# A first tile of 90 rows, earlier constants, small products between the first pairs, and routing in groups of 10, 4 and 2 tiles

## The chip, the core and the metric

The kernel runs on one NeuronCore of a Trainium2 chip: TensorE (PE in the profile, its weight loads PEld), VectorE (DVE), ScalarE (ACT), GpSimd (POOL) and SyncE (SP, which here only issues DMAs). The metric is device time in microseconds of one execution; lower is better.

## The reference

Talking-heads attention over 4 batches, 12 heads, 448 positions and 64 dimensions per head: scores are mixed between heads (`w_pre`) before the softmax, and probabilities are mixed again (`w_post`) behind it. Its output, 1,792 tokens of 768, goes to a layer of 8 experts, each token to the one with the highest cosine similarity to the experts' vectors:

```python
scores = scale * np.matmul(q, k.transpose(0, 1, 3, 2))
scores = np.einsum('bhij,hg->bgij', scores, w_pre)
scores = scores - np.max(scores, axis=-1, keepdims=True)
attn = np.exp(scores)
attn = attn / (np.sum(attn, axis=-1, keepdims=True) + 1e-09)
attn = np.einsum('bhij,hg->bgij', attn, w_post)
x = matmul(attn, v)                        # 1792 tokens of 768
logits = xn @ en.T / tau                   # xn, en: rows divided by their norms
idx = argmax(logits); gate = softmax(logits)[idx]
out[idx == e] = gate * (np.maximum(x @ w1[e], 0) @ w2[e])
```

## The kernel before, in words

**Tiles and steps.** The 448 query rows of a batch are cut into tiles of 120, 120, 120 and 90 (lines 25 and 26), 16 tiles in all. For each tile and each of 6 pairs of heads, `emit_qk` multiplies q by k (line 249); ACT or DVE moves the result from PSUM to `s` (lines 256, 258) and `place` sends it by two DMAs (line 263) to a group buffer `g`, in which 10 partitions take rows of the tile for each head, so that heads lie along the partitions. There are three such buffers (line 142); `free` says from which step a tile may be placed. Then the tile is worked off in steps of 20 rows, 10 at the end of a 90-row tile: 6, 6, 6 and 5 steps, 92 over all tiles. A step is: `emit_pre` (line 283, the mix by `w_pre`), `emit_max` (line 291, DVE), `emit_exp` (line 300, ACT), `emit_r` (lines 308 to 311, the last of them the factor `wr` on POOL), `emit_post` (lines 326 and 331, the mix by `w_post`, which also transposes), and its eviction to `a` on DVE (line 339). Pre, max and exp run two steps ahead (`LEAD`).

**The order of the work** is written out by hand: every engine and every DMA queue takes its instructions in the order in which the loop of line 784 emits them, and waits come from semaphores. In the loop the head products of later tiles are put in as `due` (line 208) says: one pair a step, three in two steps near the end, all of them by step `OPEN` = 79. Behind a tile's last step, its values products (`emit_av`, line 352), the evictions to `xT` and `xs` on ACT (lines 364, 382), the logits (line 370, lines 402 to 407 on DVE), the sum of squares (line 394) and the store to `x_tok` (line 389, SP) follow in the next tile's steps (the lists `acts`, `dves`, `pes`, `avs`, `bg`).

**Ahead of the loop** (lines 746 to 777) q, k and small constants are asked for, eight small products of ones keep PE occupied, ten pairs of head products (`N0`) are made, eight more small products follow, then pre, max and exp of steps 0 and 1. The chain that divides the experts' vectors by their norms (`embed`) runs in steps 0 to 11, three pieces a step.

**Routing.** At step 79 `open_right` frees the memory of q, k and s, opens that of the weights and asks for four weight tiles. From there `early` and `gate_value` run in the loop, two and three pieces a step: the one-hot of 12 tiles (`NE`), its prefix sums on POOL, ranks, index products, and a gather of expert 0's first 128 rows. From step 80, one half of a weight tile is split per step into a high part (line 567, ACT) and a remainder (line 568, DVE). Behind the loop come the last tile's values and logits, routing of three tiles (12 to 14) and then of the last one, while expert 0's first pass (`ffn_tok`, lines 616 to 640) fills PE in portions (`SA`). The gate values of the last four tiles are worked out inside that pass (lines 934 to 941), stored to `g_tok` from ACT's queue (line 467) and gathered; then expert 0's second pass (`st_b`) and experts 1 to 7 follow.

## Time and profile before

| | |
|---|---|
| Time before | 746.73 us, median of 3 runs (736.13 to 749.99) |
| Profiled execution | 745.5 us, span 743.6 us |
| PE busy | 693.0 us (93% of the span) |
| DVE, ACT, POOL busy | 464.0, 392.1, 118.0 us |
| PE in tenths, 40 slices of 18.6 us | 6699999999999999998988969999999999999984 |
| PEclk in tenths, same slices | 9999999999999999999989989999999999999998 |

A digit of the last two lines is the share of one slice: 9 is 90% or more. The slices of the start (6, 6), of the loop's end (8, 9, 8, 8, behind slice 18) and of the passage to the experts (6) are the ones in which PE isn't full; the last two are the kernel's end. Busy time of PE grows when its granted clock falls, since the same products take longer. "PEq", "SPq" and the like are the sequencers of the engines.

### The profile page before, as it was taken

The numbers are of one execution on the slowest core, as the hardware profiler recorded it, in microseconds if no ns is written. First come the engines' busy times: TensorE is split into PE (matmuls) and PEld (weight loads), VectorE is DVE, ScalarE is ACT, GpSimd is POOL, SyncE is SP. The second block draws the span as 40 slices with busy tenths as digits, with TensorE's granted clock in tenths as the row PEclk, the third lists the DMA queues.
The fourth block names the chain that finished last, engine by engine and source line by source line (L and its number), as shares of the span: only waits on it lengthen the run. The fifth ranks groups of instructions, "written<-read, shape, count | busy, mean of one in ns | idle before, by whom it ended". The sixth has DMA issues, their size and how long they took to land. (4 is left out here: it accounts for less than half of the span.)

```text
span 743.6 us, 25975 instructions
## 1 busy us (share of the span) xinstructions
PE 693.0 (93%) x11122; PEld 565.6 (76%) x11122; DVE 464.0 (62%) x1085; ACT 392.1 (53%) x766; POOL 118.0 (16%) x179
## 2 busy tenths in 40 slices
PE   6699999999999999998988969999999999999984
PEld 3366676676776767765767658999999999999973
DVE  3596666566666666666885555676765656565661
ACT  2565677477766666665544425445353635353540
POOL 9011001010010100101111204312112130201000
PEclk9999999999999999999989989999999999999998
DMA  6855556565556655655322364676767676665760
GB/s 238 269 156 171 168 156 186 153 190 170 156 162 191 192 172 158 194 181 182 100 51 79 86 232 153 181 264 192 240 190 238 191 257 208 200 212 195 222 207 14
DMA packets 55412, 133.06 MB, mean 179 GB/s; under 512 B 6519, under 2 KB 31239, under 8 KB 55296
## 3 DMA queue, kind: packets, MB, share of 16 engines
q1 hardware_dynamic: 50964, 117.65, 51.2%
q0 software_dynamic: 3520, 12.44, 5.1%
q8 instruction: 88, 1.44, 0.8%
q10 hardware_dynamic: 812, 1.30, 0.5%
q14 instruction: 28, 0.23, 0.1%
HBM read 81.64 MB, written 12.20 MB: 126 GB/s over the span
## 5 line engine op out<-in xcount | busy, mean ns | idle before, releaser
L291 DVE TENSOR_REDUCE mn<-p_p 128x1 f32<-128x448 f32 (+1 forms) x182 | 105.3, 618 | 100.9 <-PE p_p L283 100.6
L567 ACT ACTIVATE wh<-raw_w 128x768 fp32r<-128x768 f32 (+2 forms) x132 | 115.0, 904 | 52.3 <-DMA raw_w<-w 48.4
L568 DVE TENSOR_TENSOR wl<-raw_w,wh 128x768 fp32r<-128x768 f32 (+2 forms) x132 | 130.8, 1026 | 13.5 <-ACT wh L567 10.3
L326 PEld LDWEIGHTS p_m<-wr,e 64*64 64x64 f32 x4320 | 96.2, 136 | 54.1 <-issue 49.3
L256 ACT ACTIVATE s<-p_q 128x896 f32<-128x896 f32 x91 | 83.4, 917 | 97.9 <-PE p_q L249 97.9
L300 ACT ACTIVATE e<-p_p,mn 128x448 f32<-128x448 f32 (+1 forms) x182 | 113.7, 629 | 40.6 <-DVE mn L291 36.2
L326 PE MATMUL p_m<-wr,e 64*64 64x60 f32 x4320 | 99.6, 223 | 10.6 <-DVE a L339 5.7
L249 PE MATMUL p_q<-k,q 64*64 64x448 f32 x768 | 95.0, 567 | 9.3 <-ACT s L256 7.2
L339 DVE COPY a<-p_m 128x420 f32<-128x420 f32 (+1 forms) x184 | 98.2, 575 | 5.3 <-PE p_m L331 5.1
L352 PE MATMUL p_av<-a,v 128*64 128x120 f32 (+1 forms) x1536 | 97.0, 272 | 0.0
L966 PE MATMUL p_h<-xh,wh 128*128 128x256 f32 x336 | 96.6, 288 | 0.0
L966 PE MATMUL p_h<-xh,wl 128*128 128x256 f32 x336 | 94.8, 282 | 0.0
L966 PE MATMUL p_h<-xl,wh 128*128 128x256 f32 x336 | 94.5, 281 | 0.0
L283 PE MATMUL p_p<-g,wpre_sb 64*64 64x448 f32 (+1 forms) x712 | 90.8, 549 | 2.2 <-DMA g<-s 1.5
L311 POOL TENSOR_TENSOR wr<-wpost_sb,r 128x120 f32<-128x120 f32 (+1 forms) x92 | 35.7, 388 | 331.9 <-DVE r L310 292.1
L352 PEld LDWEIGHTS p_av<-a,v 128*64 128x64 f32 x1536 | 77.4, 140 | 10.6 <-issue 5.2
L984 PE MATMUL p_o<-wh,hh 128*128 128x384 f32 x224 | 75.7, 338 | 0.0
L984 PE MATMUL p_o<-wl,hh 128*128 128x384 f32 x224 | 74.9, 334 | 0.0
L984 PE MATMUL p_o<-wh,hl 128*128 128x384 f32 x224 | 74.9, 334 | 0.0
L968 ACT ACTIVATE hh<-p_h 128x512 fp32r<-128x512 f32 x28 | 16.7, 598 | 101.7 <-PE p_h L966 88.5
L966 PEld LDWEIGHTS p_h<-xl,wh 128*128 128x128 f32 x336 | 63.6, 189 | 0.0
L966 PEld LDWEIGHTS p_h<-xh,wl 128*128 128x128 f32 x336 | 63.2, 188 | 0.0
(210 smaller groups left out, 954.6 us busy)
## 6 DMA issues: line engine op xcount, KB each, us to landing
g<-s SPq DMA_DIRECT2D x138, 210.0 KB
raw_w<-w SPq DMA_DIRECT2D x54, 512.0 KB
raw_w<-w SPq DMA_DIRECT2D x72, 384.0 KB
g<-s SPq DMA_DIRECT2D x48, 157.5 KB
q<-qT SPq DMA_DIRECT2D x16, 384.0 KB
v<-vP SPq DMA_DIRECT2D x16, 384.0 KB
k<-kT SPq DMA_DIRECT2D x24, 224.0 KB
x_tok<-xs SPq DMA_DIRECT2D x12, 360.0 KB
```

The source lines that it names most:

```text
L249: T.matmul(p[r][64 * w:64 * w + 64, :S], q_sb[t][64 * r:64 * r + 64, a, w, :], k_sb[t // 4, a][64 * r:64 * r + 64], start=True, stop=True)
L256: A.activation(out=o, in_=i, func=ACTF.Copy)
L283: T.matmul(p[w][64 * x:64 * x + 64, :S], wpre_sb[64 * w:64 * w + 64 - 4 * w], g[64 * w:64 * w + 64 - 4 * w, m + x if nx == 2 else m], star ...
L291: V.tensor_reduce(out=mn[q, c:c + 1], in_=p[u][q, :S], op=ALU.max, axis=AX.X, negate=True)
L300: A.activation(out=e[q, c], in_=p[u][q, :S], func=ACTF.Exp, bias=mn[q, c:c + 1], accum_out=sums[q, c:c + 1])
L326: T.matmul(pm[x][q[c], u * 210 + jt * 60:u * 210 + jt * 60 + 60], e[q[x], u, jt * 128 + 64 * c:jt * 128 + 64 * c + 64], wr[q[x], u], start ...
L339: V.tensor_copy(out=a[:, :, m + x] if n == 2 else a[:, :, m, x], in_=src if n == 2 else src[:, :, 0])
L352: T.matmul(p[64 * r:64 * r + 64], v_sb[t // 4][:, jt, (2 * a + r) * D:(2 * a + r + 1) * D], a_sb[t % 2][:, c:c + n], start=jt == 0, stop=j ...
L567: A.activation(out=h[:, c], in_=r[:, c], func=ACTF.Copy)
L568: lo = lambda: eng.tensor_tensor(out=l[:, c], in0=r[:, c], in1=h[:, c].bitcast(F32), op=ALU.subtract)
L966: T.matmul(p[:, f], lt[:, c], rt_[:, k], start=(k == 0 and i == 0), stop=(k == KD - 1 and i == 2))
L984: T.matmul(p[:, :384], lt[:, k, c], rt_[:, m], start=(k == 0 and i == 0), stop=(k == KF - 1 and i == 2))
```

## The change

The tiles of batch 0 are taken in the order 90, 120, 120, 120 rows (`TILES`, `SZ`); the other batches keep theirs. Group buffers are dealt out by a list (`which`), and `free` follows from it. The first tile's q is loaded in two parts with its k tiles between; the experts' vectors and `w_pre` are asked for first, and squared and scaled on ACT ahead of the pairs; pieces of `embed` run between the pairs, one of them on POOL, with three Newton rounds where there were four. Fourteen small products stand ahead of the pairs, three behind each of the first nine, ten ahead of the first post; DVE takes most of the pairs' evictions; eleven pairs are made, pre of steps 0 and 1 ahead of the last of them. `OPEN` goes from 79 to 83. From `OPEN` on, the second half of each eviction to `a` is on ACT. The routing of ten tiles starts in the loop at step 67, the gather and transposes of the first rows at step 84, the routing of four tiles at step 88, and two tiles are left behind the loop. Seven half tiles of weights are split in the loop where there were twelve, five behind it. The split of the first rows comes behind the eviction of the step. The gate values of the last six tiles are worked out inside the second pass, whose end (`fin`, `scatter`) is held until expert 1's first products. `g_tok` is stored from SP's queue. The x tiles have one buffer where they had two. Lengths are read from `SZ[t]` throughout (left out below).

```diff
-NE = 12
+TILES = [(b, ti) for b in range(B) for ti in ((3, 0, 1, 2) if b == 0 else range(4))]
+SZ = [SIZES[ti] for _, ti in TILES]
+NE = 10
...
-N0 = 10
-NWAIT = 8
+N0 = 11
 XW = 128 + E
-OPEN = 79
+OPEN = 83
+SPL = 7
 NW = 4
-NWARM = 8
-SA = (1, 1, 1, 1, 1, 3, 3)
+NWARM = 14
 NSLOT = E * 2 + MAXO
...
-        for _ in range(4):
+        for _ in range(3):
...
-            G_.dma_start(out=wpre_sb, in_=wpre)
...
-            V.tensor_scalar(out=wpre_sb, in0=wpre_sb, scalar1=0.125, scalar2=None, op0=ALU.mult)
...
+            G_.dma_start(out=wpre_sb, in_=wpre)
+            A.activation(out=ej, in_=em, func=ACTF.Square, accum_out=es)
+            A.activation(out=wpre_sb, in_=wpre_sb, func=ACTF.Copy, scale=0.125)
+            yield
...
-            A.activation(out=ej, in_=em, func=ACTF.Square, accum_out=es)
...
-            V.tensor_scalar(out=em, in0=em, scalar1=en_n[:, 0:1], scalar2=None, op0=ALU.mult)
+            G_.tensor_scalar(out=em, in0=em, scalar1=en_n[:, 0:1], scalar2=None, op0=ALU.mult)
...
-            n = [min(NPAIR * t + NPAIR, NPAIR * t + s + 11 - first[t]) for t in range(NTL) if s > first[t] - 11]
+            n = [min(NPAIR * t + NPAIR, NPAIR * t + s + 11 - first[t]) for t in range(2, NTL) if s > first[t] - 11]
             return min(NTL * NPAIR, max(N0 + s + 1, NTL * NPAIR + 3 * (s - OPEN) // 2, *n))
...
-            back = 4 if t % 4 == 3 else 2 if t % 4 == 2 else 3
-            return first[t - back + 1] - 1 - LEAD if t >= back else 0
-
+            same = [u for u in range(t) if which[u] == which[t]]
+            return first[same[-1] + 1] - 1 - LEAD if same else 0
+
+        which = [2 if ti == 3 else (t + 1) % 2 if b == 0 else (b + ti) % 2 for t, (b, ti) in enumerate(TILES)]
...
-            Y.dma_start(out=q_sb[t], in_=qT[t // 4, :, t % 4])
+            b, ti = TILES[t]
+            for c in [slice(0, 2), slice(2, NPAIR)] if t == 0 else [slice(0, NPAIR)]:
+                Y.dma_start(out=q_sb[t][:, c], in_=qT[b, :, ti, c])
+                if t == 0:
+                    for a in range(c.start, c.stop):
+                        load_k(0, a)
...
-                    V.tensor_copy(out=a[:, :, m + x] if n == 2 else a[:, :, m, x], in_=src if n == 2 else src[:, :, 0])
+                    o, i = (a[:, :, m + x], src) if n == 2 else (a[:, :, m, x], src[:, :, 0])
+                    if x and s >= OPEN:
+                        A.activation(out=o, in_=i, func=ACTF.Copy)
+                    else:
+                        V.tensor_copy(out=o, in_=i)
...
-            for _ in range(3):
-                yield
-            p = ps_s.tile([128, 512], F32, tag="s", name="p_g")
+            yield from wait()
+            p = bank("p_g")
             T.transpose(p[:n, :128], g, id_sb)
...
-            for ti in range(4):
+            for ti, late in [(ti, late) for late in range(2) for ti in range(4)]:
                 r0 = 2 if ti == 3 else 0
                 c = slice(STARTS[ti] + r0, STARTS[ti] + SIZES[ti])
-                A.dma_start(out=g_tok.rearrange("(b s) o -> b (s o)", s=S)[t0 // 4:(t0 + n) // 4, c],
-                            in_=gt_[ti:n:4, r0:SIZES[ti]])
+                ts = [t for t in range(t0, t0 + n) if TILES[t][1] == ti and (t > 3) == late]
+                if not ts:
+                    continue
+                Y.dma_start(out=g_tok.rearrange("(b s) o -> b (s o)", s=S)[TILES[ts[0]][0]:TILES[ts[-1]][0] + 1, c],
...
-                V.tensor_tensor(out=xl[o], in0=src, in1=xh[o].bitcast(F32), op=ALU.subtract)
+
+                def split():
+                    A.activation(out=xh[o], in_=src, func=ACTF.Copy)
+                    V.tensor_tensor(out=xl[o], in0=src, in1=xh[o].bitcast(F32), op=ALU.subtract)
+                if pool is xa_p:
+                    return split
+                split()
...
                 if ks[0]:
-                    fin(n)
-            scatter(ix, o)
+                    fin(n) if held is None else held.append(lambda n=n: fin(n))
+            scatter(ix, o) if held is None else held.append(lambda: scatter(ix, o))
...
-            th = gate_thr(rt, 0, NE)
-            yield from gate_oh(rt, 0, NE, th)
-            yield from route_early()
+            th = gate_thr(re, 0, NE)
+            yield from gate_oh(re, 0, NE, th)
+            yield from route_early(bank, free_bank)
+            routed.append(now[0])
+
+        def routed_bank():
+            while not routed or routed[0] == now[0]:
+                yield
+            yield from free_bank()
+
+        def mid():
+            n = NG - NE
+            th = gate_thr(rt, NE, n)
+            yield
+            yield from gate_oh(rt, NE, n, th)
+            yield from prefix(NE, NG)
+            p = ps_s.tile([128, 512], F32, tag="s", name="p_rm")
+            rank(p, NE, n)
+            yield
+            pairs_m.extend((yield from place(rt, p, NE, n)))
+
+        def first_x():
             first_rows["x"] = gather(xa_p, idx_a)
-            for _ in range(4):
-                yield
-            first_rows["t"], first_rows["f"] = emit_xT(xa_p, [first_rows["x"]])
-            for f in first_rows["f"]:
-                f()
+            first_rows["g"] = gather_g(xa_p, idx_a)
+            yield
+            yield
+            first_rows["t"], f = emit_xT(xa_p, [first_rows["x"]])
+            for h in f:
+                tops.append(h())
                 yield
                 yield
 
+        pairs_m, tops, routed = [], [], []
         bg_at(OPEN, open_right)
-        for i in range(2 * KD):
-            bg_at(ns - 2 * KD + i, lambda i=i: w_split(V, 2, lambda lo: bg_at(ns - 2 * KD + i + 1, lo)))
-        side = {}
+        for i in range(SPL):
+            bg_at(ns - SPL + i, lambda i=i: w_split(V, 2, lambda lo: bg_at(ns - SPL + i + 1, lo)))
 
         for t in range(NTL):
-            b, ti = divmod(t, 4)
...
-        started = []
+        pes_at = set(pes)
 
         V.memset(ones_sb, 1.0)
         load_q(0)
-        for a in range(NPAIR):
-            load_k(0, a)
-        consts()
-        G_.memset(gb[0][:4], 0.0)
-        p_w = ps_m.tile([128, 512], F32, tag="m", name="p_w")
-        for _ in range(NWARM):
-            T.matmul(p_w[:, :128], ones_sb, ones_sb, start=True, stop=True)
+        load_q(1)
         ge = embed()
         next(ge)
-        for g in gb[1:]:
+        V.memset(gb[2][:4], 0.0)
+        consts()
+        next(ge)
+        for g in gb[:2]:
             G_.memset(g[:4], 0.0)
-        load_q(1)
+        p_w = ps_a.tile([128, 512], F32, tag="a", name="p_w")
+
+        def warm(n):
+            for _ in range(n):
+                T.matmul(p_w[:, :128], ones_sb, ones_sb, start=True, stop=True)
+        warm(NWARM)
         pend = []
         for i in range(N0):
-            pend.append(emit_qk(i, V if i % 2 else A, i % 2 == 1))
+            if i == N0 - 1:
+                emit_pre(0, ps_m)
+                emit_pre(1, ps_q)
+            pend.append(emit_qk(i, V if i in (1, 2, 3, 4, 5, 6, 7, 9) else A, i % 2 == 1 or i == N0 - 1))
+            if i < N0 - 2:
+                warm(3)
             if i:
                 pend.pop(0)()(A if i <= NPAIR else Y)
+            if i == 8:
+                load_q(2)
+            if 6 < i < N0 - 1:
+                for _ in range(4):
+                    next(ge, None)
+        next(ge)
+        next(ge)
+        emit_max(0)
+        emit_exp(0)
         pend.pop()()()
-        load_q(2)
+        emit_max(1)
+        emit_exp(1)
+        next(ge)
         for jt in range(4):
-            load_v(0, jt)
-        for _ in range(NWAIT):
-            T.matmul(p_w[:, :128], ones_sb, ones_sb, start=True, stop=True)
-        for s in range(LEAD):
-            emit_pre(s, s == 1)
-        for s in range(LEAD):
-            emit_max(s)
-            emit_exp(s)
-            if s == 0:
-                run(emit_r(0))
+            bg_at(jt // 2, lambda jt=jt: load_v(0, jt))
+        warm(10)
+        run(emit_r(0))
         qk_n = N0
         held = []
         placed = N0
         evict = None
-        ea = None
-        gv = None
+        gens = []
         for s in range(ns):
             cr = emit_r(s + 1) if s + 1 < ns else iter(())
             evs = []
+            ev = emit_post(s) if s == 0 else None
             want = due(s)
             assert want - qk_n < 3
-            if qk_n < want and s:
...
+            while tops:
+                tops.pop(0)()
...
-            evict = emit_post(s)
+            evict = ev or emit_post(s)
...
                     next(ge, None)
-            if s == OPEN:
-                ea = early()
-                gv = gate_value(rt, 0, NE)
-            if ea and s < ns - 1:
-                for _ in range(2):
-                    next(ea, None)
-            if gv and s > OPEN + 1:
-                for _ in range(3):
-                    next(gv, None)
+            now[0] = s
+            if s == first[NE + 1] + 3:
+                gens += [(early(), 2), (gate_value(re, 0, NE, bank, routed_bank), 2)]
+            if s == OPEN + 1:
+                gens += [(first_x(), 1)]
+            if s == first[NG + 1] + 1:
+                gens += [(mid(), 2)]
+            for g, n in gens:
+                for _ in range(n):
...
-        run(ea)
-        run(gv)
         LT = NTL - 1
+        evict()
+        emit_xT_evict(LT - 1, 1)
+        for f in tops:
+            f()
+        for g, _ in gens[:-1]:
+            run(g)
         px.close()
         ps_h = ctx.enter_context(tc.tile_pool(name="ps_h", bufs=2, space=PSUM))
-        first_rows["g"] = gather_g(xa_p, idx_a)
...
-        evict()
-        emit_xT_evict(LT - 1, 1)
-        steps_of(st_a, SA[0])
+        steps_of(st_a, 1)
+        for a in range(3):
+            emit_av(LT, a)
+        run(gens[-1][0])
         emit_xlog(LT - 1, 1)
+        emit_xT_evict(LT, 0)
         emit_lgc(LT - 1, 1)
         emit_x(LT - 1, 1)
         store_x(LT - 1)
-        emit_sq(LT - 1)
-        for a in range(3):
-            emit_av(LT, a)
-        emit_xT_evict(LT, 0)
-        steps_of(st_a, SA[1])
+        emit_sq(LT - 1, rt)
+        w_split(V, 2)
         for a in range(3, 6):
             emit_av(LT, a, ps_m, "m")
+        steps_of(st_a, 1)
         emit_xT_evict(LT, 1)
-        run(gate_oh(rt, NE, 3, gate_thr(rt, NE, 3)))
-        run(prefix(NE, LT))
-        steps_of(st_a, SA[2])
+        w_split(V, 2)
+        w_split(V, 2)
         emit_xlog(LT, 0)
+        steps_of(st_a, 1)
         emit_x(LT, 0)
-        emit_lgc(LT, 0)
-        p_rk = ps_s.tile([128, 512], F32, tag="s", name="p_rk")
-        rank(p_rk, NE, 3)
-        pairs = run(place(rt, p_rk, NE, 3))
-        steps_of(st_a, SA[3])
+        emit_lgc(LT, 0, rt)
         emit_xlog(LT, 1, ps_m, "m")
         emit_x(LT, 1)
-        emit_lgc(LT, 1)
-        emit_sq(LT)
+        emit_lgc(LT, 1, rt)
+        emit_sq(LT, rt)
         store_x(LT)
-        p_ix = ps_a.tile([128, 512], F32, tag="a", name="p_ix")
-        steps_of(st_a, SA[4])
-        index(p_ix, pairs, True, False)
         ax.close()
         pools["b"] = ctx.enter_context(tc.tile_pool(name="w2", bufs=1))
         mp = ctx.enter_context(tc.tile_pool(name="mp", bufs=2))
-        run(gate_oh(rt, LT, 1, gate_thr(rt, LT, 1)))
+        late_lo = []
+        w_split(V, 2, late_lo.append)
+        w_split(V, 2, late_lo.append)
+        run(gate_oh(rt, NG, 2, gate_thr(rt, NG, 2)))
+        for f in late_lo:
+            f()
         late_lo = []
         for _ in range(4):
             w_split(V, 1, late_lo.append)
-        steps_of(st_a, SA[5])
+        steps_of(st_a, 3)
+        run(prefix(NG, NTL))
         xb = ps_x.tile([128, 512], F32, tag="x", name="xb")
-        rank(xb, LT, 1)
-        run(prefix(LT, NTL))
-        pairs = run(place(rt, xb, LT, 1))
-        steps_of(st_a, SA[6])
-        index(p_ix, pairs, False, True)
+        rank(xb, NG, 2)
+        pairs = run(place(rt, xb, NG, 2))
+        steps_of(st_a, 4)
+        p_ix = ps_a.tile([128, 512], F32, tag="a", name="p_ix")
+        index(p_ix, pairs_m + pairs, True, True)
         iv = rt.tile([128, 2 * E], F32, name="iv")
...
-        gv = gate_value(rt, NE, 4)
         for f in fill:
-            steps_of(st_a, 4)
+            steps_of(st_a, 3)
             f()
-            steps_of(gv, 10)
         for _ in st_a:
             pass
-        run(gv)
-        rows_of(0, x=False)
-        rows_of(1, x=False)
-        st_b = ffn_tok(xT, w1p[0], w2p[0], gg[0][0], idx_s[:, 1:2])
+        gg[0] = [mp.tile([128, 1], F32, tag="gg", name="gg", bufs=6)]
+        held = []
+        st_b = ffn_tok(xT, w1p[0], w2p[0], gg[0][0], idx_s[:, 1:2], held)
         xT, fill = emit_xT(mp, xg[1])
-        rows_of(2)
+
+        def four():
+            for _ in range(4):
+                yield
+
+        gv = gate_value(rt, NE, NTL - NE, lambda name: ps_s.tile([128, 512], F32, tag="s", name=name), four)
+        rows_of(2, g=False)
         for i, _ in enumerate(st_b):
             if i % 3 == 0 and fill:
                 fill.pop(0)()
             if i >= 11 and i % 2:
                 w_split(V)
-
+            if i > 1:
+                next(gv, None)
+        run(gv)
+        gather_g(mp, cols(0)[0], gg[0][0])
+        rows_of(1, x=False)
+        rows_of(2, x=False)
...
+                if q == 1:
+                    while held:
+                        held.pop(0)()
```

## Rows read from the trace of the kernel before

**Rows 1.** The windows view: stretch, its length, busy us (instructions) of PE, PEld, DVE, ACT, POOL; PEclk; DMA share; GB/s.
```profile
0.00:40.00 40.00, 28.24 (x392) 14.88 (x394) 19.81 (x55) 16.66 (x32) 19.06 (x21) 1.00 0.75 249
...
300.22:340.71 40.49, 39.32 (x1000) 26.95 (x990) 25.64 (x67) 28.05 (x63) 3.87 (x10) 1.00 0.61 187
336.00:396.00 60.00, 52.38 (x1199) 38.12 (x1201) 45.71 (x147) 30.39 (x77) 9.89 (x28) 0.91 0.37 114
346.90:393.55 46.65, 39.60 (x919) 29.48 (x913) 38.55 (x126) 23.23 (x62) 7.37 (x25) 0.89 0.38 118
360.00:380.00 20.00, 17.13 (x368) 12.64 (x372) 18.91 (x67) 10.41 (x29) 1.91 (x6) 0.88 0.25 72
393.55:442.43 48.88, 38.45 (x369) 30.55 (x359) 26.37 (x96) 17.02 (x31) 6.74 (x9) 0.93 0.39 130
440.00:445.00 5.00, 3.03 (x13) 2.69 (x14) 2.13 (x11) 0.42 (x2) 1.03 (x1) 0.83 0.00 0
```

**Rows 2.** The timeline of the start: start us, us, engine, line, op, tiles, count, [idle before <-releaser].
```profile
1.05 3.78 PE L754 MATMUL p_w<-ones_sb 128*128 128x128 f32 x16 [1.05 <-DVE ones_sb L746]
...
14.38 1.73 PE L249 MATMUL p_q<-k,q 64*64 64x448 f32 x16 [1.47 <-ACT s L256]
...
17.34 1.73 PE L249 MATMUL p_q<-k,q 64*64 64x448 f32 x16 [1.23 <-ACT s L256]
...
19.01 2.05 PE L770 MATMUL p_w<-ones_sb 128*128 128x128 f32 x16
...
22.56 0.98 PE L283 MATMUL p_p<-g,wpre_sb 64*64 64x448 f32 x8 [1.50 <-DMA g<-s]
...
32.40 0.14 DVE L104 TENSOR_SCALAR es<-es 8x1 f32<-8x1 f32 x1 [2.41 <-ACT ej L177]
```

**Rows 3.** The windows view, one microsecond of the start.
```profile
16.00:17.00 1.00, 0.12 (x4) 0.00 (x0) 0.85 (x2) 0.62 (x1) 1.00 (x1) 1.00 0.64 233
```

**Rows 4.** The timeline of POOL, the factor `wr` that closes a step.
```profile
28.94 0.39 POOL L311 TENSOR_TENSOR wr<-wpost_sb,r 128x120 f32<-128x120 f32 x1 [2.49 <-DVE r L310]
34.62 0.39 POOL L311 TENSOR_TENSOR wr<-wpost_sb,r 128x120 f32<-128x120 f32 x1 [5.29 <-DVE r L310]
...
143.08 0.39 POOL L311 TENSOR_TENSOR wr<-wpost_sb,r 128x120 f32<-128x120 f32 x1 [2.94 <-PE p_q L249]
...
292.39 0.29 POOL L311 TENSOR_TENSOR wr<-wpost_sb,r 128x60 f32<-128x60 f32 x1 [3.06 <-DVE r L310]
...
346.90 0.39 POOL L311 TENSOR_TENSOR wr<-wpost_sb,r 128x120 f32<-128x120 f32 x1 [5.80 <-DVE r L310]
...
393.55 0.70 POOL L311 TENSOR_TENSOR wr<-wpost_sb,r 128x60 f32<-128x60 f32 x1 [2.88 <-DVE r L310]
```

**Rows 5.** The timeline of the loop's end, ACT and PE.
```profile
352.61 0.63 ACT L567 ACTIVATE wh<-raw_w 128x512 fp32r<-128x512 f32 x1 [3.92 <-DMA raw_w<-w]
...
353.65 0.96 PE L370 MATMUL p_x<-ien,xT 128*120 128x136 f32 x6 [3.04 <-ACT xT L364]
```

**Rows 6.** DVE's lines, 336 to 396 us: xcount | busy us, mean ns | idle before <-releaser.
```profile
L291 DVE TENSOR_REDUCE mn<-p_p 128x1 f32<-128x448 f32 (+1 forms) x24 | 13.8, 614 | 6.9 <-PE p_p L283 6.9
L339 DVE COPY a<-p_m 128x420 f32<-128x420 f32 x24 | 13.0, 583 | 0.0
L568 DVE TENSOR_TENSOR wl<-raw_w,wh 128x512 fp32r<-128x512 f32 x10 | 6.9, 686 | 2.6 <-DMA raw_w<-w 2.6
```

**Rows 7.** ACT's lines of the same stretch.
```profile
L300 ACT ACTIVATE e<-p_p,mn 128x448 f32<-128x448 f32 (+1 forms) x24 | 15.0, 629 | 17.2 <-DVE mn L291 16.9
```

**Rows 8.** The timeline of PE behind the pair loop.
```profile
398.75 1.29 PE L326 MATMUL p_m<-wr,e 64*64 64x60 f32 x22 [1.77 <-DVE a L339]
...
432.83 0.53 PE L635 MATMUL p_o<-wh,hh 128*128 128x384 f32 x1 [1.78 <-ACT wh L567]
...
441.97 0.27 PE L459 MATMUL p_g<-id_sb,gate 128*4 128x128 f32 x1 [3.73 <-DVE gate L454]
```

**Rows 9.** The timeline of PE inside step 28.
```profile
131.70 0.28 PE L326 MATMUL p_m<-wr,e 64*64 64x60 f32 x5 [2.54 <-issue]
```

98 lines of the change are left out of this document (54 added, 44 removed).

## The prediction

> **What bounds the kernel now.** I read the page first: TensorE (PE) is busy 693.0 of 743.6 us, so time can be won only where PE idles or runs at its lower clock. The windows by stage show four places [rows 1]. From 0 to 40 us PE is busy 28.2 of 40. In steps 70 to 80 it is busy 39.3 of 40.5 at clock 1.00: bound by PE. In steps 81 to 91 (346.9 to 393.6) it is busy 39.6 of 46.7 at clock 0.89, while DVE is busy 38.6. After the pair loop, up to expert 0's second pass (393.6 to 442.4), it is busy 38.5 of 48.9 at 0.93. From there on the page's slices show PE full until the last pass, which the change leaves alone. Then I read the timeline of the start, the POOL rows that mark each step, the waits, and DVE's lines at the loop's end.
>
> A row of POOL's factor `wr` marks each step: steps 1, 2, 30, 68, 81 and 91 in [rows 4]; the borders 300.22 and 340.71 in [rows 1] are those of steps 70 and 80.
>
> The start: the first pre product begins at 22.56, after a wait of 1.50 on the placing DMAs (g<-s) [rows 2], which run at 233 GB/s with a share of 0.64 [rows 3]. Then step 2 takes 5.68 us (28.94 to 34.62, POOL's idle there released by r) where step 1 takes 2.9 (2.49 of idle and the operation's 0.39 in its row) [rows 4]; inside it DVE stands 2.41 us behind the embedding's ACT square [rows 2]. The middle: steps 30 to 68 take 149.31 us, 3.93 each [rows 4]. The loop's end: the ten steps from 346.90 to 393.55 take 4.67 each [rows 4], although no head products are left in them after the first. DVE is busy 18.9 of 20 us from 360 to 380 [rows 1]; and once ACT waits 3.92 us for a weight DMA and PE 3.04 behind it [rows 5].
>
> **The sum's base.** The profiled execution took 745.5 us (span 743.6 and 1.9 around it), 1.2 under the median of the three runs, 746.73. I work from 745.5 and add the 1.2 at the end.
>
> **Start.** Today eight small products take 3.78 us at the low rate, and eight later ones 2.05, 0.256 each [rows 2]. Fourteen ahead of the first pair cost 3.78 + 6 x 0.256 = 5.3 and end near 6.4 (7.7 if the last six run at the first rate too), so the earlier q part and constants (both landed before that) buy nothing for PE. A pair of head products is 1.73/2 = 0.87; three small products add 0.77, so pairs come every 1.64 us where two now take 3.0 (14.38 to 17.34) [rows 2]. Ten pairs end at 6.4 + 9 x 1.64 + 0.87 = 22.0. Placement is no longer last: twelve DMAs of 157.5 KB instead of 210 are 1.9 MB, 8.1 us at 233 GB/s instead of 10.8, and pair 5 is evicted near 17. So pre(0) comes at 22.0 for 22.56: 0.5 gained. The eight small products ahead of pre (2.05) are replaced by ten ahead of post, in a wait. The embedding's chain leaves DVE's queue of the first steps for POOL, ACT and DVE's idle time during the pairs: step 2 falls from 5.68 to step 1's 2.9, 2.8 gained. A first tile of five steps brings the values product a step earlier, 0.2. Together **-3.5** (-6 if the pairs keep today's 1.5; +1 if the small products run slow and the chain lands elsewhere).
>
> **The middle.** Tile order, group buffers and the single-buffered x tiles change no count of products; a tile's store has three steps, 11.8 us, before its buffer is wanted, so 0. The first ten tiles' routing moves into steps 67 to 82. Its price: DVE is busy 45.7 us from 336 to 396 [rows 1]; maxima 13.8, evictions 13.0 and weight remainders 6.9 [rows 6] leave 12.0, small operations, routing for the most part. For ten tiles of twelve at most 10 us. The cover is DVE's idle time in PE-bound steps, 14.9 us in ten [rows 1], 1.5 a step; 0.7 a step is wanted. I charge 1.5 (0 to 10), for index products that wait in PE's queue.
>
> **Loop end.** The last head product moves from step 79 to 83, and one pair a step replaces 1.5, so steps 70 to 82 stay at 3.93 (51.1 us). Step 83 has two pairs, near 4.9. In steps 84 to 90 DVE is relieved of routing and of half of each eviction; 0.58 a step goes to ACT (no row shows ACT on this shape; 0.63, its exponential of 448, is the upper bound [rows 7], DVE's own 0.58 the value taken). ACT then has 2 x 0.63 of exponentials, some 0.4 for their sums, 0.63 and 0.58 for weights and evictions, and 0.5 of x: 3.4. DVE has 1.2 + 0.6 + 0.7 + some 0.8. PE has 3.93 - 0.98 = 2.95. With hand-overs I take 3.7 a step (3.4 to 4.67, today's): 25.9. Sum 51.1 + 4.9 + 25.9 = 81.9, and 1.5 for routing makes 83.4, against 393.55 - 300.22 = 93.3 now [rows 1, 4]: **-9.9**. The 3.92 us ACT wait goes inside that: weights are now asked for two steps ahead of their first use, not one.
>
> **Tail.** The values' gate is worked out inside the second pass, so PE's 3.73 us wait for it goes [rows 8], and with it one stretch near half clock (0.83 in 440 to 445 [rows 1]), some 1.7. The first rows' split comes behind the eviction, so PE's 1.77 wait on `a` goes [rows 8]. Five more half splits (0.69 each on DVE) come in, beside 22 us of PE work; I charge 1.7 (0 to 4). **-5.5** (-9 to +2). What is late next is the weight stream: PE waits 1.78 for `wh` at 432.8 [rows 8], kept. The six-tile gate, four g_tok stores on SP and five gathers on POOL come later; the held end of expert 0 needs them some 9 us after the pass, against about 6 for store and first gather, so 0; uncovered, a stall of up to 3. The Newton round that falls away is three operations of 0.17 in cover.
>
> **Sum.** 745.5 - 3.5 - 9.9 - 5.5 = 726.6, and 1.2 gives **728**, 2.5% below the median. 2% of it is 15 us, about what a measurement of this kernel tells from no change.
>
> **Rivals.** *The weight stream takes the place of routing.* Weights are asked for from step 83, near 351 us (300.2 - 3.5 + 13 x 3.93, and 3 for the memory to come free), against 347 now, when step 81's factor is made [rows 4], while the tail begins 13 us sooner, so the stream has 17 us less. If the second pass then waits for the last `wh` as PE does at 432.8, the loop's gain is lost there: 728 + 10 = 738. For: that wait is last in its queue today. Against: the DMA engines are far from full (share 0.39 over the whole tail [rows 1]). Chance 0.25.
>
> *Evictions stuck behind weights on ACT: slower.* From step 83 half of each eviction is issued on ACT, in order with `wh`. Today one late weight held ACT for 3.92 and PE for 3.04 [rows 5]. If each of the seven splits meets such a wait, 7 x 3.9 = 27 us: 728 + 27 = 755. It decides if a weight lands over two steps (7.4 us) after its issue. Against: the splits behind it today met none of that length, and four tiles are asked for at once. The Trainium skill, "TensorE: Matmul & The Clock Gate", Architectural detail, calls ACT and DVE strict FIFO; rows 5 agree. Chance 0.06.
>
> *The clock comes back wholly.* If PE is fed without gaps from 347 to 442, the low stretches go as well: (1 - 0.89) x 46.7 = 5.1 and (1 - 0.93) x 48.9 = 3.4, less the 1.7 counted and some 0.6 of overlap: 6 more, 722; with the start at its better end, 719. The same skill page (HAM oscillation) says that gaps bring the lower clock and steady work restores the higher; the 3.73 us of idle ahead of 441.97 [rows 8], with 0.83 in the five us around it [rows 1], agrees. By that rule the small products at the start guard the clock; the row there reads 1.00 despite 11.8 us of idle, so in my sum they gain nothing. Chance 0.14.
>
> *It does not do what it says:* the idle of 2.54 us at 131.7 [rows 9] ("issue", released by nothing shown) isn't addressed; if another appears, 4 us with its clock. This sits in every case's width.
>
> **Numbers.** Forecast 0.55, 719 to 737 by its bounds; weight stream 0.25; clock 0.14; ACT 0.06. The range 716 to 744 leaves out the ACT case and the ends of the others. Faster than 731.8: two thirds of the forecast (0.37), the clock case (0.14) and 0.02: 0.53. Slower than 761.7: 0.04. The rest, 0.43, is within 2%.
>
> **What will show it.** Right: pre(0) near 22, step 2 under 3.5 us; steps 70 to 83 near 3.93 and the last ones near 3.7, DVE under 18 of 20 us; no ACT wait of over 2 us on `raw_w`; PE going from expert 0's first pass into its second without a wait on `gate`. Wrong: steps 67 to 82 over 4.3 (routing not covered); PE waits on `wh` growing past 5 us in the tail; `a` waiting on ACT.

## The result and the profile after

The changed kernel takes **734.34 us** (median of 20 runs, 727.51 to 743.5); the kernel before took 742.35 beside it (20 runs). The ratio is 0.9876, 95% interval 0.9841 to 0.9910: 1.2% faster, where I forecast 728 and 2.5%. A second comparison with the same kernel (`again`, below) gave 0.9932 (0.9899 to 0.9964). So the sign held, and the size was half of the forecast in the one and under a third in the other. These ratios, and the means below, leave out the executions that lie more than 1.5% above the fastest of their kernel, where the granted clock is mostly lower too.

The profiled execution of the changed kernel took 729.82 us (span 728.0), against 745.5 before: 15.7 less, more than the runs show. It lies 4.5 under its own median, the one before 3.2 above the 742.35: 7.7 of the 15.7 is the draw of the two executions. First, where the 15.7 lies, by the same marks as before the change. POOL's timeline, the factor `wr` that closes steps 2, 12, 30, 68, 70, 81 and 91:

```profile
33.63 0.39 POOL L322 TENSOR_TENSOR wr<-wpost_sb,r 128x120 f32<-128x120 f32 x1 [4.78 <-DVE r L321]
...
74.12 0.39 POOL L322 TENSOR_TENSOR wr<-wpost_sb,r 128x120 f32<-128x120 f32 x1 [2.95 <-PE p_q L259]
...
143.54 0.39 POOL L322 TENSOR_TENSOR wr<-wpost_sb,r 128x120 f32<-128x120 f32 x1 [3.55 <-DVE r L321]
...
294.18 0.29 POOL L322 TENSOR_TENSOR wr<-wpost_sb,r 128x60 f32<-128x60 f32 x1 [3.06 <-DVE r L321]
...
302.55 0.39 POOL L322 TENSOR_TENSOR wr<-wpost_sb,r 128x120 f32<-128x120 f32 x1 [0.64 <-DVE r L321]
...
348.80 0.39 POOL L322 TENSOR_TENSOR wr<-wpost_sb,r 128x120 f32<-128x120 f32 x1 [4.91 <-PE p_p L294]
...
386.19 0.59 POOL L322 TENSOR_TENSOR wr<-wpost_sb,r 128x60 f32<-128x60 f32 x1 [3.16 <-DVE r L321]
```

They answer to [rows 4] and the borders in [rows 1]. Two marks of the kernel before that were not shown are step 12 and the first product of the regular experts (1 to 7):

```profile
69.21 0.39 POOL L311 TENSOR_TENSOR wr<-wpost_sb,r 128x120 f32<-128x120 f32 x1 [4.36 <-DVE r L310]
...
464.35 0.28 PE L966 MATMUL p_h<-xh,wh 128*128 128x256 f32 x1
```

The latter comes at 448.82 in the changed kernel. Stretch by stretch, the changed kernel less the one before, in us: to step 12 **+4.9**; 12 to 30 -4.5 (before lost the 2.54 of [rows 9] here, and half clock behind it); 30 to 70 +1.9; 70 to 81 -0.4; 81 to 91 **-9.3**; 91 to the regular experts **-8.2**; from there -0.1. Sum -15.6. (The first thirteen steps are not quite the same work: those of the change hold 10 rows fewer, as its fifth step is a short one. From step 22 on the two are level.)

The windows by stage (columns as in [rows 1]) are, in order, the start, steps 81 to 91, 360 to 380 us, step 91 to expert 0's second pass, and the five us around PE's longest wait in the tail:

```profile
0.00:40.00 40.00, 38.46 (x505) 23.49 (x506) 26.83 (x72) 15.54 (x33) 18.98 (x23) 1.00 0.71 218
348.80:386.19 37.39, 35.07 (x926) 26.15 (x921) 27.21 (x77) 26.54 (x69) 6.05 (x13) 1.00 0.43 133
360.00:380.00 20.00, 19.33 (x512) 14.30 (x506) 13.29 (x35) 13.65 (x38) 4.32 (x8) 1.00 0.54 175
386.19:428.68 42.49, 35.77 (x368) 30.47 (x361) 23.08 (x65) 18.84 (x34) 6.59 (x10) 0.92 0.54 177
415.00:420.00 5.00, 3.62 (x14) 3.53 (x15) 2.31 (x6) 2.17 (x3) 2.17 (x2) 0.71 0.93 283
```

At the loop's end PE now runs at 1.00 (0.89 before) and DVE from 360 to 380 is busy 13.3 us instead of 18.9. In the start PE looks busier, 38.5 of 40, but most of what came in is small products. PE's waits in the whole execution, the largest groups (us in total, how often, the longest):

```profile
PE p_m L337 <- issue: 5.1, 5, 3.2
PE p_o L653 <- DVE hl L647: 4.9, 4, 2.9
PE p_m L337 <- ACT a L352: 1.6, 1, 1.6
...
PE p_h L634 <- DVE wl L581: 1.3, 1, 1.3
...
PE p_h L634 <- ACT wh L580: 0.7, 1, 0.7
```

No wait on `gate` is left [rows 8]; a long wait on `hl`, the remainder of expert 0's hidden values, is new. It is read from PE's and DVE's timelines behind the loop:

```profile
413.14 0.34 PE L653 MATMUL p_o<-wh,hh 128*128 128x384 f32 x1
416.38 0.45 PE L653 MATMUL p_o<-wh,hl 128*128 128x384 f32 x1 [2.90 <-DVE hl L647]
```

```profile
411.45 0.17 DVE L966 TENSOR_TENSOR iv<-p_ix,ie 128x16 f32<-128x16 f32 x1 [2.78 <-PE p_ix L528]
...
411.74 3.56 DVE L581 TENSOR_TENSOR wl<-raw_w,wh 128x768 fp32r<-128x768 f32 x4
...
415.63 0.69 DVE L647 TENSOR_TENSOR hl<-p_t,hh 128x512 fp32r<-128x512 f32 x1
```

DVE stands 2.78 us for the indices, then works off four weight remainders kept back until then, and only then makes `hl`, for which PE stands. At 415 to 420 the granted clock is 0.71.

In the start SP's queue (its issues, with the time that each group took) is full from 18.7 to 53.5 us: 34.1 of 34.8.

```profile
22.61 9.75 SPq L274 DMA_DIRECT2D g<-s  x8
32.41 0.97 SPq L245 DMA_DIRECT2D v<-vP  x2
...
35.85 2.22 SPq L245 DMA_DIRECT2D v<-vP  x2
38.17 13.85 SPq L274 DMA_DIRECT2D g<-s  x10
```

Before, the four loads of `v` were issued at 26.74, ahead of the loop; now they stand behind eight more placing DMAs. Two idle times of PE come later:

```profile
54.00 0.51 PE L337 MATMUL p_m<-wr,e 64*64 64x60 f32 x19 [3.23 <-issue]
...
61.40 0.78 PE L367 MATMUL p_av<-a,v 128*64 128x90 f32 x14 [1.48 <-issue]
```

### The profile page after: what moved, and what is told of

Same layout as the page of the kernel before. It is cut to its first block, busy times and chain, and to the rows that moved or that the text cites. A ratio compares the mean times of both kernels' runs of the same rounds, so it can differ in the third digit from the quotient of the medians.

```text
span 728.0 us, 26113 instructions
## 1 busy us (share of the span) xinstructions
PE 693.6 (95%) x11192; PEld 569.6 (78%) x11192; DVE 462.2 (63%) x1069; ACT 393.5 (54%) x774; POOL 118.5 (16%) x179
## 3 DMA queue, kind: packets, MB, share of 16 engines
q1 hardware_dynamic: 51320, 117.98, 52.4%
q8 instruction: 89, 1.46, 0.8%
## 5 line engine op out<-in xcount | busy, mean ns | idle before, releaser
L267 ACT ACTIVATE s<-p_q 128x896 f32<-128x896 f32 (+1 forms) x89 | 80.8, 909 | 110.1 <-PE p_q L259 96.8
L581 DVE TENSOR_TENSOR wl<-raw_w,wh 128x768 fp32r<-128x768 f32 (+2 forms) x132 | 130.7, 1026 | 10.4 <-ACT wh L580 10.0
L337 PEld LDWEIGHTS p_m<-wr,e 64*64 64x64 f32 x4320 | 94.2, 135 | 49.1 <-issue 43.4
L311 ACT ACTIVATE e<-p_p,mn 128x448 f32<-128x448 f32 (+1 forms) x182 | 113.7, 629 | 26.4 <-DVE mn L302 22.4
L337 PE MATMUL p_m<-wr,e 64*64 64x60 f32 x4320 | 96.6, 221 | 8.5 <-issue 5.1
L354 DVE COPY a<-p_m 128x420 f32<-128x420 f32 (+1 forms) x175 | 94.2, 577 | 9.9 <-PE p_m L342 7.4
L367 PE MATMUL p_av<-a,v 128*64 128x120 f32 (+1 forms) x1536 | 94.5, 266 | 2.2 <-issue 1.5
L367 PEld LDWEIGHTS p_av<-a,v 128*64 128x64 f32 x1536 | 74.6, 136 | 10.9 <-issue 5.4
```

Of the source, the lines that this page charges most:

```text
L267: A.activation(out=o, in_=i, func=ACTF.Copy)
L311: A.activation(out=e[q, c], in_=p[u][q, :S], func=ACTF.Exp, bias=mn[q, c:c + 1], accum_out=sums[q, c:c + 1])
L337: T.matmul(pm[x][q[c], u * 210 + jt * 60:u * 210 + jt * 60 + 60], e[q[x], u, jt * 128 + 64 * c:jt * 128 + 64 * c + 64], wr[q[x], u], start ...
L354: V.tensor_copy(out=o, in_=i)
L367: T.matmul(p[64 * r:64 * r + 64], v_sb[t // 4][:, jt, (2 * a + r) * D:(2 * a + r + 1) * D], a_sb[t % 2][:, c:c + n], start=jt == 0, stop=j ...
L581: lo = lambda: eng.tensor_tensor(out=l[:, c], in0=r[:, c], in1=h[:, c].bitcast(F32), op=ALU.subtract)
```

## The experiments

Each is the changed kernel with one edit, except start_old, which puts back the whole start, and best1 and best2, which join edits. The kernel before ran beside each of them on the same chip. Its mean there was 741.6 us for again, v_spread, no_small and rest_first, 743.4 for v_ahead, start_old, evict_dve and gate_between, 742.7 for open79, best1 and best2, and 746.1 for open79_late. So a **gain** below is the difference of two means on one chip, with its standard error in brackets. The change itself gained 9.2 us in the first measurement and 6.8 (1.2) in again.

I split a mean in two: **clock**, (1 - mean granted clock) x span, which is at most what PE lost at half clock, and **rest**. In again the kernel before has 741.6 (13 executions) = 13.9 + 727.8, the changed one 734.8 (10) = 11.0 + 723.8. So of the 6.8 us 2.9 are clock and 3.9 waits and work.

**again**: no edit.

> The changed kernel once more, nothing edited. In its first profile PE waited 3.23 us at 54.0 and 1.48 at 61.4 with no releaser shown, while 16 KB instruction blocks (instruction DMA queue) were landing, and 3.41 us at half clock followed. Theory A, such waits come from instruction blocks that land late behind data transfers and so move from execution to execution: the waits over 1 us named issue stand at other places or are fewer, factor wr of step 12 comes between 69 and 74 us. Rival, they are fixed by the order of the work: 3.2 us near 54 and 1.5 near 61 again, wr of step 12 at 74.1 within 0.5. Both: step 91 follows step 70 after 83 to 85 us, median near 734.

736.12 median, ratio 0.9932 (0.9899 to 0.9964), profiled execution 728.08. The two waits stood at the same instructions:

```profile
53.15 0.51 PE L337 MATMUL p_m<-wr,e 64*64 64x60 f32 x19 [2.96 <-issue]
...
59.17 0.78 PE L367 MATMUL p_av<-a,v 128*64 128x90 f32 x14 [1.72 <-issue]
```

So the order of the work sets their place, as the rival says. Their size is not fixed: the wait before the first of these two products is 2.41 us in evict_dve, 1.17 in open79_late and 0.62 in gate_between, which leave the start alone too. The half clock behind them moves as well: none followed here, and step 12 came at 71.89. Steps 70 to 91 took 83.7 us again (301.05 to 384.71).

**v_spread**

```diff
-            bg_at(jt // 2, lambda jt=jt: load_v(0, jt))
+            bg_at(jt, lambda jt=jt: load_v(0, jt))
```

> The four loads of the first values, 384 KB each, are asked for one a step in steps 0 to 3 instead of two a step in steps 0 and 1. Theory A, the PE waits of steps 7 to 10 are instruction blocks held up by a backlog of data DMAs to which these 1.5 MB at once belong: those waits (5.2 us) and the half-clock stretch behind them (1.7) shrink, step 12 comes near 69 to 70 us instead of 74.1, the time falls by 3 to 7 us against the unedited change. Rival, the backlog is that of the head products' placement (210 KB each, one and a half a step) and the values only add to it: the waits stay, step 12 within 1.5 us, time within 2 us.

733.88, ratio 0.9881 (0.9824 to 0.9939), gain 9.4 (1.8). Step 12 came at 74.0: no gain there, as the rival says. But the wait changed its name:

```profile
52.31 0.57 PE L367 MATMUL p_av<-a,v 128*64 128x90 f32 x4 [3.08 <-DMA v<-vP]
```

Asked for one a step, `v` itself is late. So `v` has no slack in this place. The profile of rest_first, whose start is that of the change, has such a wait too:

```profile
46.28 1.77 PE L294 MATMUL p_p<-g,wpre_sb 64*64 64x448 f32 x8 [3.42 <-DMA v<-vP]
```

**v_ahead**

```diff
             if i == 8:
                 load_q(2)
+                for jt in range(4):
+                    load_v(0, jt)
...
-        for jt in range(4):
-            bg_at(jt // 2, lambda jt=jt: load_v(0, jt))
```

> The first values (four loads of 384 KB) are asked for among the first pairs of head products, ahead of the placements of pairs 8 to 10 on SP's queue, as the kernel before had them ahead of its loop; nothing else. Theory, the change lost its start in SP's queue: by 35 us it has moved 7.5 MB where the kernel before had moved 8.9, the values then compete with placements in steps 2 to 7, and instruction blocks or values come late near 50 us. Then 8.5 MB or more are moved by 35 us, PE's waits near 45 to 60 us (6.3 us in three in the first profile) fall under 3, wr of step 12 comes at 68 to 70 instead of 71.9 to 74.1, time 3 to 6 us less. Rival, the placements themselves are the limit: they come later by what the values take, pre(0) or step 2 is later, step 12 stays at 72 or more, time within 2 us.

In its profile the mechanism came as expected: step 12 at 68.41 instead of 74.1 and 71.9, and one PE wait over 1 us between 38 and 55 (2.24 on g<-s) in place of two or three. From 20 to 35 us the DMAs moved 255 GB/s, where they moved 212 in the change. By 35 us 8.0 MB had been moved (7.5 in the change, 8.9 before), less than I wanted. The time: 733.48, ratio 0.9809 (0.9739 to 0.9878), gain 11.8 (2.3), 3 to 5 us more than the change's own; five executions don't tell that from nothing. Nor do all profiles agree: best1 has the same edit, and there the rival came, the placements are late, and step 12 comes at 80.4:

```profile
52.03 1.77 PE L294 MATMUL p_p<-g,wpre_sb 64*64 64x448 f32 x8 [7.80 <-DMA g<-s]
```

So that `v` behind the placements delays steps 7 to 12 is likely, not shown.

**no_small**

```diff
-            if i < N0 - 2:
-                warm(3)
```

> The three small products after each of the first nine pairs of head products are left out (the fourteen ahead of the pairs and the ten later stay). My prediction's reading, they are time that PE pays and the clock does not need them: pairs come every 1.0 to 1.4 us instead of 1.78, pre(0) waits for the placing DMAs and comes near 20 to 22 instead of 22.6, the granted clock in 0 to 40 us stays 1.00, time 0 to 3 us less. Rival, they guard the clock: a half-clock stretch appears in the first 40 us, pairs come every 1.8 us or more, pre(0) at 23 or later, time 1 to 6 us more.

Half of each theory came true. Two pairs now take 2.2 us instead of 3.56, and pre(0) waits for the placing; but the clock falls, 0.91 in 0 to 40 us. PE's timeline, and the window:

```profile
16.84 1.50 PE L259 MATMUL p_q<-k,q 64*64 64x448 f32 x8 [0.92 <-DVE s L269]
...
21.08 1.77 PE L294 MATMUL p_p<-g,wpre_sb 64*64 64x448 f32 x8 [2.73 <-DMA g<-s]
```

```profile
0.00:40.00 40.00, 33.87 (x418) 18.36 (x420) 26.50 (x71) 15.10 (x32) 18.68 (x22) 0.91 0.69 216
```

The pre product took 0.93 in the change and takes 1.77 here. So the small products do hold the clock up, against my sum. Yet the kernel is not slower: 729.98, ratio 0.9834 (0.9788 to 0.9880), against 0.9932 for again on the same chip. Its mean of 729.9 (6) is 13.7 clock + 716.2 rest, where the change has 11.0 + 723.8. The small products buy 2.7 us of clock and cost more than that. Its profile, the slowest of its six executions, does not show where: step 12 is at 74.7. That stays open.

**start_old**: start and order of the tiles as in the kernel before, the rest as changed.

```diff
-TILES = [(b, ti) for b in range(B) for ti in ((3, 0, 1, 2) if b == 0 else range(4))]
+TILES = [(b, ti) for b in range(B) for ti in range(4)]
...
-N0 = 11
+N0 = 10
...
-NWARM = 14
+NWARM = 8
...
```

> The start and the order of the tiles are those of the kernel before (120-row tile first, ten pairs, 8 and 8 small products, the embedding's chain in the first steps, values before the loop); loop end, routing and tail are those of the change. My prediction had the new start at 3.5 us faster: then this is 2 to 5 us slower than the unedited change, step 2 takes 5.7 us, step 12 comes at 69 and everything after it is as in the change. Rival, the new start loses what it wins, to transfers and PE waits in steps 7 to 10: this is 2 to 5 us faster than the unedited change, and step 12 comes at 69 with it at 72 to 74 there.

735.44, ratio 0.9827 (0.9770 to 0.9883), gain 7.7 (1.9): by neither slower than the change. Step 2 takes 5.7 us, but step 12 comes at 72.7 in its profile, as late as with the new start, so neither theory's mark was met. Its mean of 735.8 (6) is 15.8 clock + 720.0 rest, more clock and less rest than the change has in again, on another chip. My -3.5 is not there: what the new start wins or loses as a whole is too small for these runs.

**evict_dve**

```diff
-                    if x and s >= OPEN:
+                    if False:
```

> In the change, the evictions of `a` that went to ACT from step 83 on stay on DVE (0.58 us a step). My prediction, DVE is one of the limits of the loop's last steps and half the eviction on ACT relieves it: steps 84 to 91 take 0.3 to 0.6 us longer each, steps 70 to 91 85.5 to 88 us instead of 83.7, time 2 to 4 us more. Rival, with routing moved away and one pair a step those steps are bound by PE and the hand-overs: steps 70 to 91 within 1 us of 83.7, PE's wait of 1.6 us on ACT's `a` near 384 goes, time within 1.5 us.

Steps 70 to 91 took 84.0 us, the whole 732.95, ratio 0.9812 (0.9740 to 0.9884), gain 10.4 (2.0). That is the rival: moving half the evictions to ACT is worth nothing here. PE then waits 2.0 us on DVE's `a` where it waited 1.6 on ACT's.

**gate_between**: the gate of the last six tiles is worked off beside expert 0's first pass.

```diff
+        gv = gate_value(rt, NE, NTL - NE, lambda name: ps_s.tile([128, 512], F32, tag="s", name=name), lambda: iter([None] * 3))
         for f in fill:
             steps_of(st_a, 3)
             f()
+            steps_of(gv, 10)
         for _ in st_a:
             pass
+        run(gv)
...
-            if i > 1:
-                next(gv, None)
-        run(gv)
...
```

> In the change, the gate of the last six tiles is worked out beside expert 0's first pass and ended before its second, as in the kernel before, not inside the second. My prediction, this brings back the wait on gate ahead of the second pass: PE idle there for 2 to 4 us and half clock for 3.41 us behind it, 4 to 5.5 us more. Rival, the first pass has idle DVE time enough now that routing is split, or the small operations only lengthen the wait on hl: 0 to 2 us more.

```profile
430.17 0.37 PE L473 MATMUL p_g<-id_sb,gate 128*6 128x128 f32 x1 [4.00 <-DVE gate L469]
```

The wait on `gate` is back, so this reason of the prediction is right. Its price is less clear: 738.05, ratio 0.9935 (0.9893 to 0.9977), gain 5.2 (1.4), 1.6 to 4.0 us less than the change gained, but by the ratio the same as again. From step 91 to the regular experts it takes 66.6 us; the nine other profiles that leave the tail alone have 60.1 to 66.0.

**rest_first**

```diff
+        for f in late_lo[:3]:
+            f()
+        late_lo = late_lo[3:]
         iv = rt.tile([128, 2 * E], F32, name="iv")
```

> In the tail three of the four weight remainders (0.95 us each on DVE), which run after the index sum and ahead of hl, are put before that sum, into DVE's wait of 2.78 us for p_ix. Theory, PE's new wait of 2.90 us on hl at 416.4 is DVE's queue order, four remainders ahead of hl: the wait falls under 1 us, the half-clock stretch behind it goes too, expert 0's first pass ends 2 to 4.5 us earlier, time the same amount less. Rival, the weights land no earlier (ACT waits 2.55 and 3.44 us on raw_w there) and the remainders now hold the index sum: the wait moves to wh or wl of the second layer, gain 0 to 1 us.

726.75, ratio 0.9809 (0.9758 to 0.9860), gain 14.2 (1.5): 7.4 us more than again on the same chip. Step 91 to the regular experts: 57.1 us, where the profiles that leave the tail alone have 60.1 to 66.0 (62.6 and 62.1 in the two of the change). PE's longest waits in that stretch:

```profile
PE p_t L643 <- ACT ht L638: 1.4, 1, 1.4
PE p_h L634 <- DVE wl L581: 1.3, 1, 1.3
...
PE p_o L653 <- DVE hl L647: 0.7, 1, 0.7
```

The theory holds: DVE's order held `hl`. It held the weights too, which the theory did not say: SP's queue waits for the remainders (`wl`) before it issues the next weight loads. ACT's and SP's waits behind the loop, in the changed kernel and then here:

```profile
ACT wh L580 <- DMA raw_w<-w: 12.1, 7, 3.4
SPq L565 <- DVE wl L581: 22.7, 10, 5.8
```

```profile
ACT wh L580 <- DMA raw_w<-w: 6.6, 8, 2.5
SPq L565 <- DVE wl L581: 14.7, 7, 4.4
```

How much of the gain comes by the weights was not tested.

**open79** and **open79_late**

```diff
-OPEN = 83
+OPEN = 79
```

> In the change, the head products of the last tiles end in step 79 again (one and a half a step from there), weights' memory opens at 79, half evictions go to ACT from 79 on; routing and splits stay where the change put them. Theory A, most of the loop end's 9.7 us comes from routing that left DVE's queue there (evictions have been shown not to matter): steps 70 to 91 take 83 to 86 us again, time within 2 us of the unedited change. Rival B, it comes from the four steps by which the last head product was moved, since steps 81 to 91 lose PE's work and are then bound by hand-overs: steps 70 to 79 take 1 us longer each but steps 80 to 91 gain less than that, in all 88 to 93 us, time 4 to 8 us more.

740.26, ratio 0.9962 (0.9920 to 1.0005), gain 2.9 (1.4), steps 70 to 91 in 92.6 us. That looked like rival B, but the profile has one long wait that accounts for it, a gather on POOL (POOL's rows, then PE's):

```profile
365.03 1.01 POOL L600 DMA_INDIRECT gg<-g_tok,idx_a  x1 [9.75 <-DMA g_tok<-gt__6557]
366.05 0.74 POOL L322 TENSOR_TENSOR wr<-wpost_sb,r 128x120 f32<-128x120 f32 x2
```

```profile
366.51 0.80 PE L337 MATMUL p_m<-wr,e 64*64 64x60 f32 x19 [7.03 <-POOL wr L322]
```

POOL's gathers begin one step behind OPEN, so they had come four steps earlier too, and the one of the gates stood ahead of the gates' store. The second run keeps them at step 84:

```diff
-            if s == OPEN + 1:
+            if s == 84:
```

> As in the run before, the head products end in step 79, but the first gathers on POOL stay at step 84, where the change has them. That run's 92.6 us for steps 70 to 91 held one PE wait of 7.0 us for POOL's factor wr, with POOL's gather of the gates standing 9.75 us ahead of it for their store, and half clock behind it (3.4 lost). Theory A, without that wait the end of the head products does not matter: steps 70 to 91 take 82 to 85 us, time within 2 us of the unedited change. Rival B, one and a half products a step until 79 and none after still cost: 86 to 90 us, 2 to 6 us more than the unedited change.

731.25, ratio 0.9809 (0.9765 to 0.9853), steps 70 to 91 in 85.1 us: theory A, at its edge. Where the head products end costs at most 1.5 us in these steps. The gain of 14.8 (1.3) is larger than the change's own; these steps don't show why.

**best1** (v_ahead and rest_first) and **best2** (no_small besides):

> The change with two edits measured before, the first values asked for ahead of the last placements and three weight remainders put into DVE's wait for p_ix. If the two gains stand beside each other (3 us in the loop's first twelve steps, 5 us between step 91 and the first regular expert): step 12 at 68 to 70 us, 57 us from step 91 to expert 1, median 722 to 727, ratio to the kernel before 0.972 to 0.980. If the earlier steps only move the waits on weights into the tail: ratio 0.981 to 0.986.

> The same and, besides, without the three small products after each of the first nine pairs. If they are time that PE pays while transfers set the pace anyway: pre(0) 1 to 2 us earlier, step 12 within 1.5 us, ratio within 0.003 of best1's. If their 7 us count: ratio 0.004 to 0.008 lower. If they guard the clock: half-clock stretches in the first 40 us and a ratio 0.003 or more higher.

730.64, ratio 0.9773 (0.9698 to 0.9848), and 728.19, ratio 0.9809 (0.9734 to 0.9884), with three executions each in the ratio. From step 91 to the regular experts they take 56.8 and 57.1 us: that gain stands. The start's gains don't add up clearly: step 12 comes at 80.4 in best1's profile, behind the PE wait of 7.80 us shown above, and at 68.6 in best2's. Both are faster than the kernel before; three executions don't tell by how much they beat the change, and rest_first alone has the tighter evidence.

## Why the prediction was half right

**The base.** I set all gains against one execution, 745.5 us, and added 1.2 to reach the median of three. Waits and half-clock stretches that this execution happened to have were counted as gains in full. The kernel's executions spread over 736 to 754 us, and the median of twenty is 742.35, 4.4 below mine. Of the gain of 18.9 us that I forecast 8.0 came; that 728 lies only 6.3 from the result is in part luck, since the base was too high. The result lies in my range, and within the 2% to which I gave a chance of 0.43, against 0.53 for a faster kernel than that. Nor does the 737 that I gave as the forecast's upper bound come out of its terms: their upper bounds add up to 755.

**Start, -3.5: the step that failed.** By step 30 the change stands 0.5 us later than the kernel before. Pre(0) came at 22.60 (I said 22.0): a pair and its three small products take 1.78, not 1.64. The largest term was 2.8 for step 2, and 0.5 came: step 2 took 5.17, not 2.9, and 5.2 or more in all twelve profiles with this start. I had put its length down to the embedding's chain. The chain is gone from there, but the change also emits ten small products, the post of step 0 and a pair of head products ahead of pre(2), with which step 2 begins. PE's timeline, before and then after:

```profile
25.01 1.59 PE L283 MATMUL p_p<-g,wpre_sb 64*64 64x448 f32 x8 [0.71 <-ACT e L300]
```

```profile
29.60 0.93 PE L294 MATMUL p_p<-g,wpre_sb 64*64 64x448 f32 x8
```

The factor of step 2 follows 4.0 us later, at 33.63. No run undid this order alone. Then steps 2 to 12 take 40.5 us, and 36.5 to 42.0 in the seven profiles that leave this start as it is; with the old start they take 34.6 and 35.3. I priced PE and DVE there and let placement cost nothing once it was not last; I missed that `v` is moved past eight placing DMAs on SP's queue, which is full until 53 us. With `v` in front they take 33.8 in v_ahead and 32.7 in best2, but 40.8 in best1. Steps 12 to 30 give it back, which I had not forecast: 69.1 to 70.2 us in the twelve profiles with the new start, 73.9 and 74.3 in the two with the old, each of which has a wait named issue of 2.5 to 2.8 us there.

**Small products.** I let them gain nothing. By rows they hold the clock: in the first 40 us it is 1.00 in eight of the ten profiles that have them between the pairs, and 0.96 in the two where PE waits 2.7 and 4.1 us for a placement; it is 0.91 in both that lack them. With the old start it was 1.00 once [rows 1] and 0.91 once (start_old), so the 1.00 of [rows 1] was in part a draw. The rule that I weighed there, the Trainium skill's "TensorE: Matmul & The Clock Gate", HAM oscillation, by which gaps bring the lower clock and steady work keeps the higher, agrees with these rows. The time does not follow: the kernel without them is no slower.

**Middle, +1.5.** Steps 68 to 81 took 54.5 us before and 54.6 after, which looks as if routing were covered. But they hold fewer head products now, PE's lines before and then after:

```profile
L249 PE MATMUL p_q<-k,q 64*64 64x448 f32 x120 | 14.7, 559 | 0.6 <-ACT s L256 0.5
```

```profile
L259 PE MATMUL p_q<-k,q 64*64 64x448 f32 x104 | 12.8, 562 | 0.0
```

With 120 again, in open79_late, they take 57.0. So routing costs some 2 to 2.5 us here, a little more than the 1.5 that I charged.

**Loop end, -9.9.** Steps 70 to 91 took 83.6 us, forecast 83.4, part by part too: 52.4 to step 83 for 51.1 and 1.5, then 4.8 for 4.9 and 26.4 for 25.9. They took 83.2 to 86.1 in the eight further profiles that leave this stretch and the start's order of tiles alone; no ACT wait on `raw_w` is left in it. (start_old's profile took 90.4, with a PE wait of 2.5 named issue and half clock behind it.) Two of my reasons fell: half the eviction on ACT is worth nothing, and the later end of the head products 1.5 us at most. What is left is the work that left DVE's queue (13.3 of 20 us busy instead of 18.9), with the clock that came back (1.00 for 0.89). That is routing, but not routing alone: in steps 81 to 91 DVE's weight remainders fell from the 6.9 us of [rows 6] to 3.4, as five of ten half tiles went behind these steps.

```profile
L581 DVE TENSOR_TENSOR wl<-raw_w,wh 128x512 fp32r<-128x512 f32 x5 | 3.4, 687 | 0.0
```

ACT's wait of 3.92 us for a weight is gone too, and with it PE's 3.04 [rows 5], a third of the 9.7 us. No run undid routing or the splits alone, so how the gain divides between them stays open. How much of the 93.3 before belonged to that one execution was not measured either.

**Tail, -5.5.** It was -8.2 in the profiles. The wait on `gate` went and came back in gate_between, so that part was right in kind; its size is not settled. The term of 1.7 us for extra half splits was the wrong kind: not their time, their place ahead of `hl` costs, 5.0 us in rest_first's tail. I named the weight stream as late next; DVE's order came first.

**Rivals.** The weight stream did not take over: in the second pass PE meets no wait on `wh` of the size that the rival needed (0.7 on `wh` and 1.3 on `wl` in the whole execution). The stream does show under another name, and earlier. In the first pass of again PE waits for `hh`, which stands on ACT behind the split of a late weight (PE, then ACT):

```profile
420.67 0.44 PE L653 MATMUL p_o<-wh,hh 128*128 128x384 f32 x1 [2.11 <-ACT hh L646]
```

```profile
419.29 0.84 ACT L580 ACTIVATE wh<-raw_w 128x768 fp32r<-128x768 f32 x1 [2.02 <-DMA raw_w<-w]
```

PE waited for ACT's `a` once, 1.4 to 2.0 us by profile, not seven times. The clock came back at the loop's end but not in the tail (0.92).

## What to carry to other kernels

When a load is moved, follow it past everything on its issuing queue until the reader, even where the engine that you speed up doesn't wait for it today. When a step is to start sooner, look at what the new order puts ahead of its first product, not only at what it takes away. When a wait goes, look at which in-order queue has long work issued just ahead of the next thing that TensorE needs: reordering three operations gave as much here (7.4 us) as the whole change on the same chip (6.8). And take the size of a gain from several executions, not from the stalls of one.

## What the runs showed of the hardware

PE's waits named "issue" seem to go with its instruction blocks. Between 45.2 and 51.4 us of the changed kernel's profile no block of 16 KB came for PE; one, on the instruction queue (queue, packets, MB, share), lies in 51.4 to 53.0:

```profile
q1 hardware_dynamic: 189, 0.31, 62.8%
q8 instruction: 1, 0.02, 4.1%
```

PE stood until 54.00. There are 89 such blocks in the execution, 1.46 MB, some 65 bytes for each of PE's 22,384 products and weight loads, which is why I take the queue for PE's. In again the block moved between 50.0 and 50.5 us and PE's product came at 53.15; in gate_between between 51.0 and 51.5, and the product at 54.02, after a wait of 0.62. So each time the product follows 2 to 3 us behind the block. The Trainium skill, "Runtime: NRT & Kernel Launch", Instruction fetch mechanics, calls the crossing of such a block mostly hidden; here PE stood 3.23 us at one and 1.48 at another. What delays the block was not tested.

A gather that waits for its data holds what is queued on POOL behind it: 9.75 us there became 7.03 of PE (open79).
